# A retention-plus-FFN kernel on one Trainium2 core: a new hand-written order for the first 32 FFN slots, and steps over two PSUM banks merged

## The chip, the cores and the metric

The kernel runs on one core of a Trainium2 chip. The metric is device time in microseconds (us), the median of three runs; lower is better. The engines are named as the profile names them: PE (TensorE matmul) and PEld (its weight loads), DVE (VectorE), ACT (ScalarE), POOL (GpSimd) and SP (SyncE, which issues nearly all DMAs here). Each engine works through its own list of instructions in order; semaphores connect the lists.

## The reference

For 4 batches, 8 heads, 768 tokens and head size 64, a retention layer with a decay per head feeds a feed-forward network whose nonlinearity is a rational function. Everything is float32.

```python
state = gamma * state + k[t] (outer) v[t]          # 64 x 64 per head, token by token
y[t]  = scale * q[t] @ state
x = y of all heads, as [3072 tokens, 512]
h = x @ w_in                                       # 512 -> 2048
P = a[0] + a[1]*h + a[2]*h**2 + a[3]*h**3
Q = 1 + |b[0]|*|h| + |b[1]|*h**2
out = (P / (Q + 1e-6)) @ w_out                     # 2048 -> 512
```

## The kernel before

**Retention.** Tokens are taken in 24 chunks of 128 (six to a batch). For a chunk i the steps are, with the letters that the order below uses: load (four DMAs on SP's queue: v, k, kT, qT), q and v (scale qT and v by decays, one POOL step each), S (scores, k times q, on PE), M (multiply by the causal mask, DVE, out of PSUM), V (mask times v, PE), R and r (recall from the state, PE), O (outer product of k and v for the state, PE), C (add the state, DVE), s (decay it, POOL), X (round the result to the PE's fast float format, ACT: the high part xh) and Y (the remainder xl, DVE). Chunks 0 to 3 work on whole chunks of 128 tokens; from chunk 4 on a chunk is done in two halves of 64, whose scores and results lie in two PSUM banks, the tile `pair`. There is one such tile, so that S of a chunk waits for Y of the chunk before it. M, X and Y are two instructions each, one for each bank.

**FFN.** Four chunks make a block of 512 tokens; there are six blocks and 16 slices of 128 of the hidden dimension, so 96 slots. Each slot has gemm_in (letter I, `gemm_in`, L480) of 12 matmuls of 512 columns: high and low part of x against high and low part of the weight; the rational function; and gemm_out (letter Z, `gemm_out`, L536) of 12 more. For slot 0 gemm_in comes in two cuts, I0 (384 columns) and J0 (128). Between I and Z lie, per slot: a = absolute value (ACT), b = affine (ACT, or POOL where the list says `b...!`), c = linear (ACT), p = product (POOL), f = two DVE steps (L504, L505), e = two ACT steps (reciprocal square root, square), H = three DVE steps (L513, L514, L515), g = high part of the result (ACT), K = low part (POOL). I of a slot k writes one of two banks `ph`, and so it waits until H of slot k-2 has read its bank; Z of a slot waits for its K.

**Weights.** w_in and w_out come as 64-bit floats and are decoded on the chip, a tile of [128, 512] at a time, 32 tiles in all: fetch (DMA on SP), t and u (ACT), d (two DVE steps, L160 and L163), h (high part, ACT) and l (low part, POOL). Scratch for u lies in a PSUM bank that is free at that time; the name after @ says which. Slots 0 to 7 are block 0 against the first half of the hidden dimension, slots 8 to 15 block 1 against the same weights, slots 16 to 31 the same two blocks against the second half. Slots 0 to 7 need tiles 0 to 15, slots 16 to 23 tiles 16 to 31; slots 8 to 15 and 24 to 31 need no new ones. Slot 32 and the later ones belong to blocks 2 to 5.

**Who sets the order.** All instructions stand in an order written out by hand; nothing reorders them. Up to slot 31 it is the text BEGIN, one word to a step (letter and number; `fillN` is N dummy matmuls on zeros; `fetch1` the next weight tile; `loadN` a chunk; w, y and sums store and reload partial sums). An exclamation mark moves the step to its other engine: for q, v, l, p and K from POOL to DVE, for b from ACT to POOL. From slot 32 on the loop `run` gives a regular order. SP's queue is in the order of the text as well; 11 weight tiles and chunks 0 to 5 are issued ahead of BEGIN.

Of the kernel before, what the change touches and what calls it, by code (L numbers as in the profile page):

```python
# [21 lines left out]
def tile_retention_rational_ffn(  # L22
# [111 lines left out]

    def decode_low(i):
        if i >= len(tiles):
            return
# [4 lines left out]
        nc.scalar.activation(ts[i], byte, AF.Identity, bias=lcon[:, 0:1], scale=1.0 / 32)
# [24 lines left out]
    def decode_split(i):  # L167
# [5 lines left out]
        nc.scalar.copy(w[:, 0], ts[i].bitcast(F32))  # L173
# [241 lines left out]
    def mask(i, ordered=False):  # L415
        st = steps[i]
        for r in range(2):
            st["aT", r] = at.tile([P, NP, HP], F32, name="aT")
            x = nc.vector.tensor_mul(
                st["aT", r], st["pa"][r],  # L420
                causal_sb[:, :HP].unsqueeze(1).broadcast_to([P, NP, HP]),
            )
# [25 lines left out]
    def x_parts(i, kh):  # L448
        n, s = divmod(i, SPB)
        t = slice(s * P + kh * HP, s * P + (kh + 1) * HP)  # L450
        xh, xl = (y[:, :, t] for y in x_block(n))
        return pair(i)[kh][:, TB // 2 :].rearrange("p (n t) -> p n t", t=HP), xh, xl

    def x_high(i, r):
        x, xh, _ = x_parts(i, r)
        nc.scalar.copy(xh, x)

    def x_low(i, r):
        x, xh, xl = x_parts(i, r)
        nc.vector.tensor_sub(xl, x, xh.bitcast(F32))  # L460
# [51 lines left out]
    def ratio_vector(ph, p, q, s):  # L512
        nc.vector.scalar_tensor_tensor(q, q, qcon[:, 0:1], ph, ALU.add, ALU.mult)  # L513
        nc.vector.scalar_tensor_tensor(ph, p, par_sb[:, 0:1], ph, ALU.add, ALU.mult)  # L514
        nc.vector.scalar_tensor_tensor(p, q, 2.0, ph, ALU.subtract, ALU.mult, reverse0=True)  # L515
# [298 lines left out]
t0 B0 u0@ph1 d0 h0 q0 l0 fill20 S0 v0 M0 v1 fill2 O0 V0 C0 q1 O1 X0 n0 s1 S1 t1 Y0 u1@po2 C1 R1  # L814
M1 s2 d1 fill1 V1 X1 v2! h1 q2! fill1 O2 l1 Y1 S2 C2 t2 s3 R2 M2 u2@ph1 v3 d2 fill1 V2 q3 O3 X2
h2 C3 S3 Y2 t3 s4 l2 u3@po2 R3 M3 I0 v4 d3 q4 V3 h3 t4 l3 O4 X3 C4 t5 v5 u4@po2 Y3 u5@po0 d4 s5
fill4 J0 S4 a0 q5 d5 h4 I1 c0 l4 t6 f0 h5 fetch1 b0! u6@po1 l5 R4 t7 d6 a1 p0 u7@po2 M4 h6 d7 t8
fill4 V4 b1! c1 r4 l6 O5 load6 u8@po0 C5 f1 X4 p1 t9 h7 Y4 u9@po1 l7 fetch1 d8 fill6 S5 e0 R5 v6
M5 h8 H0 t10 fill2 V5 l8 e1 r5 O6 load7 q6 u10@po2 H1 fill1 I2 t11 X5 g0 fetch1 u11@po0 C6 K0 g1
d9 I3 a2 K1 c2 Y5 b2 v7 d10 h9 p2 S6 a3 fetch1 f2 R6 h10 s7 c3 l10 b3 M6 e2 d11 fill4 V6 q7 r6  # L820
O7 load8 f3 h11 p3 Z0 X6 C7 l9 e3 Y6 fetch1 s8 t12 H2 S7 l11 t13 Z1 v8 t14 H3 g2 q8 R7 K2 fetch1
I4 M7 g3 u12@half0 K3 d12 Z2 a4 u13@half0 b4 d13 fetch1 c4 p4 h12 I5 f4 h13 l12 u14@half0 e4 d14
l13 Z3 t15 H4 fetch1 a5 u15@half0 b5! c5 p5 d15 h14 I6 g4 t16 K4 f5 h15 u16@half0 fetch1 l15
l14! e5 Z4 d16 t17 H5 a6 t18 b6! V7 c6 p6 r7 h16 fetch1 O8 f6 g5 I7 l16 X7 load9 K5! e6 Y7 C8
t19 Z5 a7 H6 s9 fetch1 u17@pair0 b7! c7 v9 u18@pair1 f7 g6 I8 p7 d17 q9 fetch1 e7 K6 d18 h17 Z6
a8 u19@pair0 l17 H7 b8 fetch1 c8 p8 t20 f8 I9 g7 u20@pair1 K7 h18 d19 e8 fetch1 l18 Z7 d20 a9
t21 b9! c9 H8 p9 h20 fetch1 h19 S8 l20 w8 R8 f9 I10 g8 l19 y8 e9 K8 fetch1 M8 t22 Z8 H9 a10 t23
b10! c10 p10 u21@half0 f10 I11 g9 fetch1 K9 d21 e10 Z9 u22@half0 H10 a11 h21 fetch1 b11! c11 l21
d22 g10 I12 p11 t24 f11 u23@half0 K10 h22 fetch1 d23 e11 Z10 l22 a12 H11 u24@half0 b12! c12 p12
fetch1 t25 f12 h23 I13 g11 l23 d24 e12 K11 fetch1 t26 Z11 H12 a13 h24 b13! c13 l24 p13!  # L830
u25@half0 I14 g12 f13 t27 K12 d25 e13 Z12 a14 H13 h25 b14 l25 c14 u26@half0 p14 I15 f14 t28 g13
d26 e14 K13 Z13 a15 H14 h26 b15! c15 l26 u27@half0 f15 g14 I16 p15 t29 d27 e15 K14! Z14
u28@half0 H15 a16 h27 c16 l27 b16 f16 I17 g15 p16 t30 d28 K15 e16 Z15 a17 H16 h28 b17! c17 p17
u29@half0 f17 g16 I18 w16 K16 l28! e17 y16 Z16 t31 H17 a18 b18 c18 p18 d29 I19 g17 f18 u30@half0
h29 l29 sums0 K17! Z17 e18 d30 a19 H18 c19 b19 V8 h30 r8 p19 O9 load10 f19 g18 I20 l30 C9 e19
K18 H19 Z18 a20 v10 c20 s10 b20 f20 g19 p20 I21 q10! K19 e20 H20 Z19 a21 b21 c21 p21 g20 f21 I22
K20 e21 H21 Z20 a22 b22 c22 p22 g21 f22 I23 K21 e22 H22 Z21 X8 a23 b23 Y8 c23 p23 g22 I24 f23
u31@pair0 K22 d31 e23 Z22 a24 H23 h31 c24 l31 b24 f24 g23 p24 S9 I25 K23 e24 H24 R9 a25 Z23 b25
c25 M9 p25 g24 f25 K24 V9 y24 e25 I26 H25 r9 a26 Z24 b26 c26 p26 g25 f26 load11 O10 K25! Z25 e26
C10 X9 H26 s11 v11 I27 Y9 g26 q11 K26 S10 a27 I28 b27 c27 p27 f27 R10 a28 Z26 M10 e27 c28 H27  # L840
b28 V10 p28 r10 O11 f28 load12 g27 I29 X10 K27 Y10 e28 C11 v12 H28 S11 a29 Z27 c29 b29 f29 g28
p29 K28! R11 e29 I30 q12! M11 H29 V11 a30 r11 c30 b30! O12 load13 g29 f30 p30 I31 X11 K29 Y11
# [69 lines left out]
```

## Time and profile before

| | |
|---|---|
| median of 3 runs | 621.27 us (621.22 to 621.86) |
| the profiled execution | 621.15 us, with a span of 619.1 us |
| PE busy | 606.9 us, 98% of the span |
| DVE, ACT, POOL busy | 453.9, 441.8 and 346.5 us (73%, 71%, 56%) |
| granted TensorE clock | 1.0 throughout |
| matmuls of gemm_in and gemm_out | 1164 and 1152 |

The span is the time from the first to the last instruction of the program; the time of a run has some 2 us beside it. The busy share of PE holds the dummy matmuls too, and matmuls whose modelled end is late. The shares are averages: the first sixth of the span, where the weights are decoded and the first chunks are made, and the rest, where PE has a full list, have different limits.

### The profile page before, as it was taken

What the parts mean: (1) busy time and instruction counts of PE and PEld (TensorE: products, weight loads), DVE (VectorE), ACT (ScalarE), POOL (GpSimd) and SP (SyncE); (2) the same over time, 40 slices, a digit from 0 to 9 for tenths busy, and PEclk for the clock granted to TensorE, in tenths of its full rate; (3) what the DMA queues carried; (4) which work ended last, traced back from release to release, by engine and by line L of the source; (5) the groups of instructions that cost most, each with busy time, mean ns of one, the idle gap of its engine ahead of it and who ended that gap; (6) DMA issues with size and microseconds to landing.
All of it is one profiled execution on the core that took longest, in us unless ns stands there. A gap on an engine that the chain in (4) does not pass through costs nothing.

```text
span 619.1 us, 12618 instructions
## 1 busy us (share of the span) xinstructions
PE 606.9 (98%) x5044; PEld 487.6 (79%) x5050; DVE 453.9 (73%) x717; ACT 441.8 (71%) x723; POOL 346.5 (56%) x296
## 2 busy tenths in 40 slices
PE   8979999999999999999999999999999999999997
PEld 5757877887887788888888888888888888888886
DVE  4799899999868686766766766666767666766664
ACT  3598889998675666676666757666766667777773
POOL 4789687865654455464545545554646444444441
PEclk9999999999999999999999999999999999999999
DMA  8977265103203240420120320110301000100001
GB/s 333 387 236 266 110 239 225 48 1 136 69 2 128 70 137 1 137 69 19 53 60 1 137 69 2 69 46 25 137 10 53 1 1 1 68 1 0 2 0 68
DMA packets 24283, 52.87 MB, mean 85 GB/s; under 512 B 2721, under 2 KB 3105, under 8 KB 24225
## 3 DMA queue, kind: packets, MB, share of 16 engines
q1 hardware_dynamic: 24080, 51.94, 23.7%
q8 instruction: 39, 0.64, 0.4%
q14 instruction: 20, 0.16, 0.1%
q10 hardware_dynamic: 144, 0.13, 0.1%
HBM read 43.67 MB, written 8.39 MB: 84 GB/s over the span
## 4 chain that ended last, share of the span: by engine, by line
PE 83%; DVE 3%; issue 1%; ACT 1%; DVEq 0%; ACTq 0%
PE po L536 39%; PE ph L480 39%; PE pair L442 2%; PE pair L394 2%; PE pair L409 1%; PE pair L283 1%; DVE q L513 0%; DVE t L163 0%; DVE pair L160 0%; DVE ph L514 0%; DVE p L515 0%; DVE p L504 0%; DVE w L180 0%; DVE p L505 0%; ACT s L629 0%
## 5 line engine op out<-in xcount | busy, mean ns | idle before, releaser
L480 PE MATMUL ph<-xh,w 128*128 128x512 f32 (+2 forms) x776 | 210.0, 393 | 1.6 <-DVE p L515 1.3
L536 PE MATMUL po<-w,gh 128*128 128x512 f32 x768 | 200.1, 393 | 0.0
L499 POOL TENSOR_TENSOR q<-q,s 128x512 f32<-128x512 f32 x64 | 83.1, 1298 | 183.9 <-ACT s L498 183.9
L480 PEld LDWEIGHTS ph<-xh,w 128*128 128x128 f32 x776 | 142.9, 188 | 33.6 <-DVE p L515 4.1
L536 PEld LDWEIGHTS po<-w,gh 128*128 128x128 f32 x768 | 142.7, 188 | 30.3
L504 DVE TENSOR_TENSOR p<-ph,p 128x512 f32<-128x512 f32 x96 | 66.2, 690 | 85.4 <-ACT p L500 75.5
L536 PE MATMUL po<-w,gl 128*128 128x512 f32 x384 | 110.7, 390 | 0.0
L480 PE MATMUL ph<-xl,w 128*128 128x512 f32 (+2 forms) x388 | 103.7, 389 | 0.1
L513 DVE SCALAR_TENSOR_TENSOR q<-q,qcon,ph 128x512 f32<-128x512 f32 x96 | 71.5, 745 | 40.9 <-ACT ph L510 39.8
L492 ACT ACTIVATE q<-ph 128x512 f32<-128x512 f32 x64 | 38.3, 598 | 87.8 <-PE ph L480 87.8
L480 PEld LDWEIGHTS ph<-xl,w 128*128 128x128 f32 x388 | 72.7, 188 | 15.7 <-DVE xl L382 0.2
L509 ACT ACTIVATE s<-q,qcon 128x512 f32<-128x512 f32 x96 | 69.5, 724 | 21.0 <-POOL q L499 14.0
L536 PEld LDWEIGHTS po<-w,gl 128*128 128x128 f32 x384 | 72.1, 188 | 15.4 <-POOL gl L646 0.5
L521 POOL TENSOR_TENSOR gl<-p,gh 128x512 fp32r<-128x512 f32 x64 | 82.8, 1294 | 0.5 <-POOL q L499 0.5
L505 DVE SCALAR_TENSOR_TENSOR p<-p,con_sb,ph 128x512 f32<-128x512 f32 x96 | 71.8, 748 | 3.4
L514 DVE SCALAR_TENSOR_TENSOR ph<-p,con_sb,ph 128x512 f32<-128x512 f32 x96 | 71.9, 749 | 0.0
L515 DVE SCALAR_TENSOR_TENSOR p<-q,ph 128x512 f32<-128x512 f32 x96 | 65.9, 687 | 3.3
L510 ACT ACTIVATE ph<-s 128x512 f32<-128x512 f32 x96 | 57.8, 602 | 10.8 <-DVE p L505 1.4
L633 POOL TENSOR_TENSOR q<-q,s 128x512 f32<-128x512 f32 x31 | 40.1, 1293 | 31.5 <-ACT s L629 28.2
L498 ACT ACTIVATE s<-q,babs 128x512 f32<-128x512 f32 x64 | 52.3, 817 | 2.1
L500 ACT ACTIVATE p<-ph,con_sb 128x512 f32<-128x512 f32 x64 | 48.8, 763 | 0.0
L180 POOL TENSOR_TENSOR w<-t,w 128x512 fp32r<-128x512 f32 x30 | 39.3, 1313 | 14.5 <-ACT w L173 14.5
(75 smaller groups left out, 615.1 us busy)
## 6 DMA issues: line engine op xcount, KB each, us to landing
raw<-in_w_in SPq DMA_DIRECT2D x16, 512.0 KB, 7.5
raw<-in_w_out SPq DMA_DIRECT2D x16, 512.0 KB, 6.9
kT<-in_kT SPq DMA_DIRECT2D x24, 256.0 KB, 3.9
qT<-in_qT SPq DMA_DIRECT2D x24, 256.0 KB, 4.1
v<-in_v SPq DMA_DIRECT2D x24, 256.0 KB, 3.3
out<-o SPq DMA_DIRECT2D x23, 256.0 KB, 2.2
...
```

The costliest lines, as they stand in the source:

```text
L480: nc.tensor.matmul(ph[:, t0:t1], w1[f][:, part, kt * P : (kt + 1) * P], x[:, kt, t0:t1], start=(i == 0), stop=(i == 3 * NP - 1),)
L498: nc.scalar.activation(s, q, AF.Identity, bias=babs[:, 0:1], scale=babs[:, 1:2])
L499: nc.gpsimd.tensor_mul(q, q, s)
L504: nc.vector.tensor_mul(p, ph, p)
L505: nc.vector.scalar_tensor_tensor(p, p, par_sb[:, 1:2], ph, ALU.add, ALU.mult)
L509: nc.scalar.activation(s, q, AF.Abs_reciprocal_sqrt, bias=qcon[:, 0:1])
L510: nc.scalar.activation(ph, s, AF.Square)
L513: nc.vector.scalar_tensor_tensor(q, q, qcon[:, 0:1], ph, ALU.add, ALU.mult)
L514: nc.vector.scalar_tensor_tensor(ph, p, par_sb[:, 0:1], ph, ALU.add, ALU.mult)
L515: nc.vector.scalar_tensor_tensor(p, q, 2.0, ph, ALU.subtract, ALU.mult, reverse0=True)
L521: engine.tensor_sub(gl, p, gh.bitcast(F32))
L536: nc.tensor.matmul(o_tiles[n][tt], g_[:, tt * P : (tt + 1) * P], w2[f][:, part], start=(first and m == 0), stop=(last and m == 2),)
```

## The change

The change has four parts.

1. **A new text BEGIN.** The same steps stand in a new order on every engine. There are 20 dummy matmuls after the first twenty instead of 26. Tiles 16 to 31 are decoded later. No q, v, l, p or K step is left on DVE (before: v2, q2, q10, q12, l14, l28, p13, K5, K14, K17, K25, K28), b on POOL is down from 13 slots to 7, and three steps go from ACT to POOL: t20, t25 and h10. The two texts are, up to gemm_in of slot 12:

```
before
t0 B0 u0@ph1 d0 h0 q0 l0 fill20 S0 v0 M0 v1 fill2 O0 V0 C0 q1 O1 X0 n0 s1 S1 t1 Y0 u1@po2 C1 R1 M1
s2 d1 fill1 V1 X1 v2! h1 q2! fill1 O2 l1 Y1 S2 C2 t2 s3 R2 M2 u2@ph1 v3 d2 fill1 V2 q3 O3 X2 h2 C3
S3 Y2 t3 s4 l2 u3@po2 R3 M3 I0 v4 d3 q4 V3 h3 t4 l3 O4 X3 C4 t5 v5 u4@po2 Y3 u5@po0 d4 s5 fill4 J0
S4 a0 q5 d5 h4 I1 c0 l4 t6 f0 h5 fetch1 b0! u6@po1 l5 R4 t7 d6 a1 p0 u7@po2 M4 h6 d7 t8 fill4 V4 b1!
c1 r4 l6 O5 load6 u8@po0 C5 f1 X4 p1 t9 h7 Y4 u9@po1 l7 fetch1 d8 fill6 S5 e0 R5 v6 M5 h8 H0 t10
fill2 V5 l8 e1 r5 O6 load7 q6 u10@po2 H1 fill1 I2 t11 X5 g0 fetch1 u11@po0 C6 K0 g1 d9 I3 a2 K1 c2
Y5 b2 v7 d10 h9 p2 S6 a3 fetch1 f2 R6 h10 s7 c3 l10 b3 M6 e2 d11 fill4 V6 q7 r6 O7 load8 f3 h11 p3
Z0 X6 C7 l9 e3 Y6 fetch1 s8 t12 H2 S7 l11 t13 Z1 v8 t14 H3 g2 q8 R7 K2 fetch1 I4 M7 g3 u12@half0 K3
d12 Z2 a4 u13@half0 b4 d13 fetch1 c4 p4 h12 I5 f4 h13 l12 u14@half0 e4 d14 l13 Z3 t15 H4 fetch1 a5
u15@half0 b5! c5 p5 d15 h14 I6 g4 t16 K4 f5 h15 u16@half0 fetch1 l15 l14! e5 Z4 d16 t17 H5 a6 t18
b6! V7 c6 p6 r7 h16 fetch1 O8 f6 g5 I7 l16 X7 load9 K5! e6 Y7 C8 t19 Z5 a7 H6 s9 fetch1 u17@pair0
b7! c7 v9 u18@pair1 f7 g6 I8 p7 d17 q9 fetch1 e7 K6 d18 h17 Z6 a8 u19@pair0 l17 H7 b8 fetch1 c8 p8
t20 f8 I9 g7 u20@pair1 K7 h18 d19 e8 fetch1 l18 Z7 d20 a9 t21 b9! c9 H8 p9 h20 fetch1 h19 S8 l20 w8
R8 f9 I10 g8 l19 y8 e9 K8 fetch1 M8 t22 Z8 H9 a10 t23 b10! c10 p10 u21@half0 f10 I11 g9 fetch1 K9
d21 e10 Z9 u22@half0 H10 a11 h21 fetch1 b11! c11 l21 d22 g10 I12

after
t0 B0 u0@ph1 q0 v0 fill20 S0 v1 O0 M0 C0 fill2 V0 d0 q1 O1 X0 n0 s1 S1 h0 Y0 v2 t1 C1 R1 M1 u1@po2
s2 O2 d1 V1 q2 X1 C2 l0 S2 t2 Y1 u2@ph1 M2 v3 R2 h1 s3 d2 fill1 V2 q3 O3 X2 h2 Y2 S3 t3 v4 u3@po2 R3
M3 l1 C3 fill3 V3 d3 s4 l2 O4 X3 I0 C4 t4 q4 Y3 u4@po2 h3 d4 s5 t5 S4 l3 R4 u5@po0 J0 M4 h4 v5 d5 a0
V4 c0 r4 l4 O5 I1 C5 X4 f0 q5 t6 u6@po1 Y4 b0! h5 d6 t7 p0 S5 load6 a1 R5 u7@po2 M5 l5 e0 d7 fill2
V5 r5 t8 fetch1 H0 c1 v6 b1 load7 fill7 O6 u8@po0 p1 f1 g0 I2 h6 q6 X5 C6 e1 fetch1 Y5 l6 d8 h7 S6
a2 K0 R6 t9 M6 h8 v7 H1 fill3 V6 u9@po1 r6 c2 l7 O7 load8 b2 f2 s7 g1 fill1 I3 p2 t10 X6 d9 fetch1
K1 e2 C7 Z0 l8 a3 Y6 h9 H2 c3 q7 u10@pair0 b3 l9 fetch1 t11 d10 fill1 I4 p3 t12 f3 u11@pair1 h10! g2
u12@pair0 v8 d11 Z1 e3 l10 fetch1 d12 a4 h11 K2 t13 H3 S7 b4 l11 R7 c4 Z2 h12 s8 M7 g3 p4 f4 t14
fetch1 u13@half0 K3 I5 d13 e4 l12 H4 h13 V7 a5 r7 c5 b5! O8 load9 t15 f5 p5 I6 X7 g4 C8 e5 K4 fetch1
Y7 Z3 a6 H5 c6 b6 u14@pair0 p6 f6 I7 u15@pair1 g5 l13 d14 fetch1 e6 K5 H6 Z4 a7 b7 c7 p7 t16 f7 I8
fetch1 g6 h14 K6 d15 e7 s9 H7 l14 Z5 a8 fetch1 c8 b8 f8 h15 p8 u16@pair0 I9 g7 d16 l15 e8 fetch1 K7
t17 H8 Z6 a9 c9 b9! t18 p9 f9 fetch1 u17@pair1 I10 u18@pair0 d17 e9 h16 H9 fetch1 l16 Z7 a10 h17 g8
d18 b10 K8 g9 I11 y8 t19 l17 fetch1 c10 w8 p10 f10 u19@pair1 Z8 K9 e10 d19 fetch1 t20! a11 H10 h18
c11 Z9 l18 u20@pair0 h19 f11 b11! fetch1 t21 p11 u21@pair1 d20 I12
```

The PE steps of slots 22 to 28 show how the small retention matmuls stand among the large ones:

```
before  Z22 S9 I25 R9 Z23 V9 I26 r9 Z24 O10 Z25 I27 S10 I28 R10 Z26 V10 r10 O11 I29 S11 Z27 R11 I30 ...
after   Z22 S9 R9 I25 Z23 I26 V9 r9 O10 Z24 I27 Z25 I28 Z26 S10 R10 I29 V10 r10 O11 Z27 I30 S11 R11 I31 ...
```

2. **Steps over two banks merged.** M (from chunk 4 on), X and Y become one instruction over both banks. This holds in `run` too.

```diff
-        for r in range(2):
-            st["aT", r] = at.tile([P, NP, HP], F32, name="aT")
-            x = nc.vector.tensor_mul(
-                st["aT", r], st["pa"][r],
-                causal_sb[:, :HP].unsqueeze(1).broadcast_to([P, NP, HP]),
-            )
-            if ordered and r == 1:
-                after(x, st["recalled"])
+        aT = at.tile([P, 2, NP, HP], F32, name="aT", bufs=1)
+        for r in range(2):
+            st["aT", r] = aT[:, 1 - r]
+        x = nc.vector.tensor_mul(
+            aT, both_banks(i)[:, :, : TB // 2].rearrange("p b (n t) -> p b n t", t=HP),
+            causal_sb[:, :HP].unsqueeze(1).unsqueeze(1).broadcast_to([P, 2, NP, HP]),
+        )
+        if ordered:
+            after(x, st["recalled"])
...
-    def x_high_both(i):
-        for r in range(2):
-            x_high(i, r)
+    def x_high(i):
+        x, xh, _ = x_parts(i)          # both banks
         nc.scalar.copy(xh, x)
```

3. **An immediate in place of a per-partition constant** in the first step of H, in all 96 slots:

```diff
-        nc.vector.scalar_tensor_tensor(q, q, qcon[:, 0:1], ph, ALU.add, ALU.mult)
+        nc.vector.scalar_tensor_tensor(q, q, 1.0 + 1e-6, ph, ALU.add, ALU.mult)
```

4. **Other engines for t, h, g and the stores**, where the text marks them:

```diff
-    def decode_low(i):
+    def decode_low(i, engine=None):
...
-        nc.scalar.activation(ts[i], byte, AF.Identity, bias=lcon[:, 0:1], scale=1.0 / 32)
+        if engine is None:
+            nc.scalar.activation(ts[i], byte, AF.Identity, bias=lcon[:, 0:1], scale=1.0 / 32)
+        else:
+            engine.tensor_scalar(
+                ts[i], byte, 1.0 / 32, -15.5 / 32, op0=ALU.mult, op1=ALU.add
+            )
...
+                other = {"w": nc.vector.tensor_copy, "y": nc.scalar.copy}
+                other.update({x: nc.gpsimd for x in "bthg"})
+                more.append(other.get(word[0], nc.vector))
```

More of the change, by code (lines that the diff above doesn't have):

```diff
@@ L69, in pair @@
             pairs[i] = [both[:, r] for r in range(2)]
+            boths[i] = both
             if i >= SPB:
@@ L72, in pair, with both_banks @@
         return pairs[i]
+    def both_banks(i):
+        pair(i)
+        return boths[i]
     def u_place(i, place):
@@ L129, in tile_retention_rational_ffn, with round_to @@
     us, ts = {}, {}
+    def round_to(dst, src, engine=None):
+        if engine is None:
+            nc.scalar.copy(dst, src)
+        else:
+            engine.tensor_copy(dst, src)
     def decode_read(i, place=None):
@@ L165, in decode_join, with decode_split @@
         )
-    def decode_split(i):
+    def decode_split(i, engine=None):
         if i >= len(tiles):
@@ L365, in whole_values, with whole_x @@
                     )
-    def whole_x(i, r):
+    def whole_x(i):
         t = slice((i % SPB) * P, (i % SPB + 1) * P)
         xh, xl = (
-            y.rearrange("p (a r) t -> p a r t", r=2)[:, :, r, t] for y in x_block(i // SPB)
+            y.rearrange("p (a r) t -> p r a t", r=2)[:, :, :, t] for y in x_block(i // SPB)
         )
-        return whole_px(i, r), xh, xl
+        x = both_banks(i)[:, :, : TB // 2].rearrange("p r (a t) -> p r a t", t=P)
+        return x, xh, xl
     def whole_x_high(i):
-        for r in range(2):
-            x, xh, _ = whole_x(i, r)
-            nc.scalar.copy(xh, x)
+        x, xh, _ = whole_x(i)
+        nc.scalar.copy(xh, x)
     def whole_x_low(i):
-        for r in range(2):
-            x, xh, xl = whole_x(i, r)
-            nc.vector.tensor_sub(xl, x, xh.bitcast(F32))
+        x, xh, xl = whole_x(i)
+        nc.vector.tensor_sub(xl, x, xh.bitcast(F32))
     def px(i, kh):
@@ L446, in values, with x_parts, x_low @@
                         )
-    def x_parts(i, kh):
+    def x_parts(i):
         n, s = divmod(i, SPB)
[L450 to L455, printed above, removed]
+        xh, xl = (
+            y[:, :, s * P : (s + 1) * P].rearrange("p n (k t) -> p n k t", k=2)
+            for y in x_block(n)
+        )
+        x = both_banks(i)[:, :, TB // 2 :].rearrange("p k (n t) -> p n k t", t=HP)
+        return x, xh, xl
+    def x_high(i):
+        x, xh, _ = x_parts(i)
         nc.scalar.copy(xh, x)
-    def x_low(i, r):
-        x, xh, xl = x_parts(i, r)
+    def x_low(i):
+        x, xh, xl = x_parts(i)
         nc.vector.tensor_sub(xl, x, xh.bitcast(F32))
-    def x_high_both(i):
-        for r in range(2):
-            x_high(i, r)
-    def x_low_both(i):
-        for r in range(2):
-            x_low(i, r)
         del steps[i]
@@ L553, in store_last, with store @@
             queue.dma_start(out=dst[:, cut], in_=o[:, cut])
-    def store(n, half, which=range(SPB)):
+    def store(n, half, which=range(SPB), copy=None):
         for tt in which:
@@ L650, in load_chunk, with store_group @@
             load_by_dim(i)
-        def store_group(k, which):
+        def store_group(k, which, copy=None):
             n, f = order[k - 1]
-            store(n, f // HF, range(*which))
+            store(n, f // HF, range(*which), copy)
         emit = {
@@ L753, in run @@
                 carry(chunk + 1)
-                x_high_both(chunk)
+                x_high(chunk)
                 if not summed:
-                    x_low_both(chunk)
+                    x_low(chunk)
                 load_by_token(chunk + 2)
@@ L770, in run @@
             if part == 1 and summed:
-                x_low_both(chunk)
+                x_low(chunk)
             if plain:
@@ L813 @@
 BEGIN = """
[L814 to L842, printed above, removed]
@@ L843 @@
-e30 C12 v13 Z28 a31 H30 b31 s13 c31 p31 f31 g30 K30 e31 H31
+t0 B0 u0@ph1 q0 v0 fill20 S0 v1 O0 M0 C0 fill2 V0 d0 q1 O1 X0 n0 s1 S1 h0 Y0 v2 t1 C1 R1 M1
+u1@po2 s2 O2 d1 V1 q2 X1 C2 l0 S2 t2 Y1 u2@ph1 M2 v3 R2 h1 s3 d2 fill1 V2 q3 O3 X2 h2 Y2 S3 t3
+v4 u3@po2 R3 M3 l1 C3 fill3 V3 d3 s4 l2 O4 X3 I0 C4 t4 q4 Y3 u4@po2 h3 d4 s5 t5 S4 l3 R4 u5@po0
+J0 M4 h4 v5 d5 a0 V4 c0 r4 l4 O5 I1 C5 X4 f0 q5 t6 u6@po1 Y4 b0! h5 d6 t7 p0 S5 load6 a1 R5
+u7@po2 M5 l5 e0 d7 fill2 V5 r5 t8 fetch1 H0 c1 v6 b1 load7 fill7 O6 u8@po0 p1 f1 g0 I2 h6 q6 X5
@@ new lines @@
+C6 e1 fetch1 Y5 l6 d8 h7 S6 a2 K0 R6 t9 M6 h8 v7 H1 fill3 V6 u9@po1 r6 c2 l7 O7 load8 b2 f2 s7
+g1 fill1 I3 p2 t10 X6 d9 fetch1 K1 e2 C7 Z0 l8 a3 Y6 h9 H2 c3 q7 u10@pair0 b3 l9 fetch1 t11 d10
+fill1 I4 p3 t12 f3 u11@pair1 h10! g2 u12@pair0 v8 d11 Z1 e3 l10 fetch1 d12 a4 h11 K2 t13 H3 S7
+b4 l11 R7 c4 Z2 h12 s8 M7 g3 p4 f4 t14 fetch1 u13@half0 K3 I5 d13 e4 l12 H4 h13 V7 a5 r7 c5 b5!
+O8 load9 t15 f5 p5 I6 X7 g4 C8 e5 K4 fetch1 Y7 Z3 a6 H5 c6 b6 u14@pair0 p6 f6 I7 u15@pair1 g5
+l13 d14 fetch1 e6 K5 H6 Z4 a7 b7 c7 p7 t16 f7 I8 fetch1 g6 h14 K6 d15 e7 s9 H7 l14 Z5 a8 fetch1
@@ new lines @@
+c8 b8 f8 h15 p8 u16@pair0 I9 g7 d16 l15 e8 fetch1 K7 t17 H8 Z6 a9 c9 b9! t18 p9 f9 fetch1
+u17@pair1 I10 u18@pair0 d17 e9 h16 H9 fetch1 l16 Z7 a10 h17 g8 d18 b10 K8 g9 I11 y8 t19 l17
+fetch1 c10 w8 p10 f10 u19@pair1 Z8 K9 e10 d19 fetch1 t20! a11 H10 h18 c11 Z9 l18 u20@pair0 h19
+f11 b11! fetch1 t21 p11 u21@pair1 d20 I12 g10 e11 K10 d21 fetch1 l19 H11 Z10 a12 h20 b12! c12
+p12 t22 f12 g11 I13 fetch1 u22@pair0 K11 h21 d22 e12 l20 Z11 H12 a13 h22 b13! c13 fetch1 p13 t23
+f13 u23@pair1 I14 l22 g12 d23 e13 K12 fetch1 H13 l21 Z12 a14 h23 c14 b14! t24 p14 f14 g13 fetch1
@@ new lines @@
+I15 u24@pair0 t25! e14 d24 l23 u25@pair1 H14 K13 Z13 a15 b15 c15 p15 t26 f15 I16 h24 g14 d25 e15
+K14 l24 H15 Z14 a16 c16 b16 f16 u26@pair0 p16 g15 I17 t27 d26 K15 u27@pair1 h25 d27 q8 e16 Z15
+a17 H16 c17 b17 S8 w16 p17 f17 R8 I18 g16 l25 h27 M8 e17 y16 K16 H17 Z16 a18 v9 b18 c18 p18 t28
+f18 I19 g17 u28@half0 K17 e18 l27 H18 Z17 a19 h26 c19 l26 b19 f19 g18 p19 I20 t29 d28 K18 e19
+u29@half0 Z18 H19 a20 c20 b20 f20 t30 p20 I21 g19 d29 K19 e20 q9 H20 Z19 a21 h28 c21 l28 b21 f21
+t31 p21 I22 g20 K20 e21 Z20 H21 a22 u30@half0 c22 h29 d30 b22 I23 p22 f22 h30 g21 l29 e22 V8 l30
@@ new lines @@
+r8 a23 H22 O9 load10 K21 Z21 X8 c23 C9 b23 Y8 s10 g22 I24 f23 p23 u31@pair0 K22 d31 e23 Z22 a24
+H23 h31 b24 l31 sums0 c24 g23 p24 S9 f24 R9 I25 q10 M9 e24 K23 H24 Z23 a25 c25 g24 f25 b25 I26
+p25 y24 v10 e25 K24 V9 a26 H25 r9 O10 load11 c26 Z24 b26 f26 p26 g25 K25 C10 e26 I27 s11 H26 Z25
+a27 c27 b27 f27 X9 p27 g26 I28 Y9 v11 e27 K26 H27 Z26 a28 b28 p28 g27 c28 S10 q11 f28 R10 I29
+K27 M10 e28 H28 V10 a29 r10 b29 O11 load12 Z27 c29 p29 g28 f29 X10 K28 C11 e29 Y10 I30 v12 H29
+S11 a30 R11 c30 I31 M11 g29 f30 b30 p30 V11 K29 e30 r11 O12 load13 q12 Z28 X11 H30 a31 c31 b31
@@ L844 @@
+f31 g30 p31 Y11 K30 e31 C12 s13 H31 v13
 """
```

21 lines of the change are left out of this document (11 added, 10 removed).

## The prediction

> **What bounds the kernel now.** I took the time by stages first. The columns are the busy time of PE, PEld, DVE, ACT and POOL (with instructions), the granted clock, the DMA share and GB/s.
>
> ```profile
> 8.10:30.00 21.90, 20.03 (x303) 16.07 (x305) 16.00 (x32) 10.40 (x22) 17.07 (x18) 1.00 1.04 391
> 30.00:98.00 68.00, 62.71 (x749) 48.50 (x753) 62.94 (x104) 61.65 (x108) 55.76 (x50) 1.00 0.55 199
> 98.00:228.00 130.00, 129.87 (x966) 103.61 (x967) 111.06 (x172) 101.86 (x169) 77.79 (x66) 1.00 0.27 94
> 228.00:604.50 376.50, 376.50 (x2965) 308.26 (x2964) 255.07 (x396) 258.45 (x411) 191.57 (x158) 1.00 0.12 41
> ```
>
> From 98 us on PE has no idle time to win: 0.13 us up to slot 31, none in the loop. A new order can gain there only by making PE's own list cheaper. PE's idle time lies ahead: 1.9 us between 8 and 30 us, where the DMA engines are full (1.04), and 5.3 us between 30 and 98 us. In that stretch DVE is busy 93% of the time and ACT 91%, while PE's busy time holds dummies too. So it is DVE and ACT work with PE waiting. The chain of waits names which of the two:
>
> ```profile
> PE pair L409 <- DVE xl L460: 1.4, 1, 1.4
> PE ph L480 <- DVE p L515: 1.3, 3, 0.6
> ```
>
> The columns are total, times and longest, in us. Both releasers are DVE. What counts is when the three steps of H are through, since they open the bank for gemm_in two slots later.
>
> **Start and data.** S0 follows the same 20 dummies; the first 11 weight tiles and six chunks are queued ahead of BEGIN as before. Then load6, load7 and load8 each move on SP ahead of a fetch that they stood behind, and tiles 13 and 14 now wait behind load8, that is, until chunk 6 is done (V6, r6, O7). I cost this at nothing: t13 stands on ACT behind a4, which waits for gemm_in of slot 4, while V6 precedes I3. More than a slot covers it, with the DMA engines 55% busy. If V6 came later than that, tile 13 would be late next.
>
> **DVE, step by step.** A stretch of DVE's timeline without a gap (start, duration) gives prices from start to start:
>
> ```profile
> 75.85 0.69 DVE L160 SCALAR_TENSOR_TENSOR pair<-pair,t 128x512 uint32<-128x512 uint32 x1
> 76.63 0.69 DVE L163 SCALAR_TENSOR_TENSOR t<-raw,pair 128x512 uint32<-128x512 uint32 x1
> 77.23 0.74 DVE L513 SCALAR_TENSOR_TENSOR q<-q,qcon,ph 128x512 f32<-128x512 f32 x1
> 77.89 0.75 DVE L514 SCALAR_TENSOR_TENSOR ph<-p,con_sb,ph 128x512 f32<-128x512 f32 x1
> 78.68 0.69 DVE L515 SCALAR_TENSOR_TENSOR p<-q,ph 128x512 f32<-128x512 f32 x1
> 79.28 0.68 DVE L504 TENSOR_TENSOR p<-ph,p 128x512 f32<-128x512 f32 x1
> 80.00 0.75 DVE L505 SCALAR_TENSOR_TENSOR p<-p,con_sb,ph 128x512 f32<-128x512 f32 x1
> 80.66 0.69 DVE L646 TENSOR_TENSOR gl<-p,gh 128x512 fp32r<-128x512 f32 x1
> 81.27 0.75 DVE L460 TENSOR_TENSOR xl<-pair,xh 128x256 fp32r<-128x256 f32 x2
> ```
>
> d costs 1.38 (77.23 - 75.85), H 2.05, f 1.38, and one 512-column step such as K on DVE 0.61; I take that for q2 and v2 too. The pair of Y (x2) takes 0.75 for two; one step of 512 columns should take the 0.69 of its neighbours. So merging saves 0.06, no more, since the pair overlapped already, and a mask, a pair of the same form, likewise. One read over two banks has no row: between a gain of 0.06 and a loss of as much a step, the eleven that matter make plus or minus 0.7; I take the gain, as the 512-column rows are the nearest. X merged counts as nothing. The immediate makes L513 like L515, which has one: 0.74 to 0.69, so 0.05 per H.
>
> Two ends of H in the old order:
>
> ```profile
> 58.01 0.69 DVE L515 SCALAR_TENSOR_TENSOR p<-q,ph 128x512 f32<-128x512 f32 x1
> ...
> 70.89 0.69 DVE L515 SCALAR_TENSOR_TENSOR p<-q,ph 128x512 f32<-128x512 f32 x1
> ```
>
> H2 ended at 58.7. Counted in the two texts, DVE now has ahead of it d for 10 tiles in place of 12 (2.76), f for 3 slots in place of 4 (1.38), no q2 and v2 (1.22), 10 merged M and Y (0.6) and three immediates (0.15): 6.1 less. With DVE's other gaps as they were, H2 ends at 52.6.
>
> H4 ended at 71.6. One d less (1.38), q2 and v2 (1.22), 11 merges (0.66), five immediates (0.25): 3.5 less, 68.1. But between H3 and H4 DVE idled for these:
>
> ```profile
> DVE pair L160 <- ACT pair L150: 1.9, 2, 1.1
> DVE aT L419 <- PE pair L394: 0.3, 1, 0.3
> ```
>
> The 0.3 is M7 waiting for R7; 0.8 of the 1.9 is d12, whose u12 waits for the half bank that M7 frees. The new order decodes u11 and u12 in `pair` ahead of S7, so this 1.1 goes. The other 1.1, u13, still follows M7 and stays. H4 ends at 67.0; 68.1 if nothing goes, 65.9 if all goes.
>
> **PE from there.** The price of a gemm (chain, start and length) and places in PE's timeline:
>
> ```profile
> 106.50 2.72 PE po L536 x12
> ```
> ```profile
> 94.01 0.62 PE L536 MATMUL po<-w,gh 128*128 128x512 f32 x2
> ...
> 97.88 1.20 PE L480 MATMUL ph<-xh,w 128*128 128x512 f32 x4
> ...
> 109.06 1.07 PE L480 MATMUL ph<-xh,w 128*128 128x512 f32 x4
> ...
> 150.99 1.98 PE L536 MATMUL po<-w,gh 128*128 128x512 f32 x8
> ...
> 155.13 1.20 PE L480 MATMUL ph<-xh,w 128*128 128x512 f32 x4
> ...
> 179.74 1.98 PE L536 MATMUL po<-w,gh 128*128 128x512 f32 x8
> ...
> 197.01 1.20 PE L536 MATMUL po<-w,gh 128*128 128x512 f32 x4
> ```
>
> A gemm takes 2.72. Z7, S8 and R8 take 97.88 - 94.01 = 3.87, so S and R in a row cost 1.15, of which 0.13 is PE's only idle time here: 1.02. Z17, V8, r8 and O9 take 4.14: V, r, O cost 1.42.
>
> In the new order I4 starts with H2's end, 52.6; Z1 at 55.3; after S7 R7, Z2 at 59.0; I5 at 61.8. V7 r7 O8 end at 65.9, and I6 waits for H4 until 67.0. From I6 to I12 lie 13 gemms, 35.4 us, and no small work: I12 at 102.4. Later H stay ahead by the same count (before H7 DVE has three d, l14, K5, q2 and v2 less). The old I12 starts at 109.06 with S8 and R8 done, which the new list does after Z15; the place to compare is 107.9. **First term: 5.5 us gained** (4.4 and 6.6 at the two ends for H4). K and l back on POOL delay Z by up to one POOL step, covered by the gemm_in that stands between H and Z.
>
> **Second term, the small matmuls.** From Z22 to Z25 the old order has five gemms with S9, R9, V9, r9 and O10 one by one between them: 197.01 - 179.74 = 17.27, less 13.60, is 3.67. As S R and V r O they cost 1.02 + 1.42 = 2.44; 1.23 gained for three breaks, 0.41 a break. Chunks 10 and 11 lose one break each, R behind S. **2.0 us in all,** and on the path, since PE is full there. What could take it back is the set of sums: loaded after Z22 and not slot 19, added by y24 on DVE (four steps) ahead of Z24. Two gemms and V9 r9 O10 lie between Z23's start and Z24, 6.9 us; that covers them.
>
> The rest is nothing: the merged steps and immediates of the loop lie under a PE busy 376.50 of 376.50 us. The sum is 7.5. The profiled execution took 621.15, 0.12 below the median of the runs; 621.15 - 7.5 = 613.7 (rounded up), its own range 612.5 to 615.
>
> **Rivals.**
>
> *ACT takes DVE's place.* By line, in the stretch from 30 to 140 us (count, busy, mean ns):
>
> ```profile
> L142 ACT ACTIVATE t<-raw,lcon 128x512 uint32<-128x512 uint8 x25 | 19.0, 763 | 1.1 <-POOL w L180 0.8 <-DVE w L180 0.2
> L173 ACT CAST w<-t 128x512 fp32r<-128x512 f32 x24 | 14.6, 615 | 0.1
> ```
>
> Ahead of e15 ACT has five t, two u and three h less, but four b more, back from POOL: six steps net, at 0.62 to 0.76 some 3.7 to 4.6 us, where DVE sheds nearly 9 by H7 already. If ACT keeps all its idle gaps, e15, and with it H15 and I17, come 3.7 earlier, of which S8 R8, still to do, take 1.15: 2.5 gained, with the second term 4.5, so 616.6. For it: ACT's 91%. Against: part of its gaps are waits for PE and shrink with them. 0.20.
>
> *The waits vanish.* If DVE and ACT keep up, PE's 7.3 us of idle time go, and six dummies:
>
> ```profile
> 37.36 1.47 PE L602 MATMUL fill<-zeros 128*128 128x512 bf16 x5
> ```
>
> At 0.29 each these are 1.8; with the second term 11.1, so 610.0. For it: the new text puts dummies at V5, O6 and V6, where small matmuls follow each other's mask. Against: DVE's list still holds 90% of the stretch. 0.16.
>
> *Slower, by POOL.* No row shows POOL reading bytes, as t20 and t25 now do. The nearest are one input and two inputs of 512 columns:
>
> ```profile
> 31.52 1.30 POOL L180 TENSOR_TENSOR w<-t,w 128x512 fp32r<-128x512 f32 x1 [0.94 <-ACT w L173]
> 32.80 0.77 POOL L626 TENSOR_SCALAR s<-q,babs 128x512 f32<-128x512 f32 x1
> ```
>
> I take 0.77, the row of the same operation. t20 stands ahead of b11 and p11, and so of e11, H11 and I13; t25 likewise of slot 15. POOL is 60% busy from 98 us on, so 2.2 of a slot's 5.4 us cover a slow step. At 7 us each the loss, 2 x (7 - 0.8 - 2.2) = 8.0, passes the gain; at 8 us the time is 613.7 + 10 = 623.7. Nothing in the profile speaks for steps so long; 1.30 would cost nothing. 0.06.
>
> *A hole slows PE.* The first dummies, after an idle PE:
>
> ```profile
> 1.19 6.99 PE L602 MATMUL fill<-zeros 128*128 128x512 bf16 x20 [1.19 <-DVE lcon L784]
> ```
>
> They take 0.35 each, against 0.29 later, so an idle PE restarts slowly, 1.2 us over twenty. With six dummies fewer, a hole of 3 us and a restart would cost some 4 of the 7.5: 617.9. My largest hole is the 1.1 at I6, and after the 1.4 of the waits above the clock stayed 1.00. 0.03. The Trainium skill (TensorE: Matmul & The Clock Gate, Why this matters for your kernels) sets the limit at PE-idle gaps of about 3 us, after which the clock falls to half; the trace agrees in that 1.4 us did no harm, and no run here shows 3. By that rule alone nothing changes below such a hole.
>
> **How the numbers follow.** My forecast has 0.50; 0.05 is left for an early lead that both full lists lose again before slot 16, which ends within 0.2% (1.2 us, about what a measurement of this kernel can tell from no change). Faster: 0.50 + 0.20 + 0.16 + 0.03 = 0.89; same 0.05; slower 0.06. The range goes from the case without waits, 610.0 less half a microsecond, to the slow-PE case, 618.
>
> **What would show it.** DVE without any l, q, v, p or K step; the first step of H at 0.69; masks of 512 columns at 0.69. H2 ending near 52.6, I6 starting near 67 behind the last step of H4, I12 near 102.4, PE without idle time after that; R9 right behind S9; POOL's t near 0.77. I am wrong if ACT's steps, not DVE's, precede the gaps of PE between 50 and 100 us, if I12 comes after 106, or if PE waits again after 110.

## The result, and the profile after

| | before | after |
|---|---|---|
| median | 621.4 us (621.22 to 621.86) | 614.14 us (613.99 to 615.09) |
| ratio | | 0.9885, 95% interval 0.9868 to 0.9902 |
| the profiled execution | 621.15 us, span 619.1 | 613.99 us, span 612.2 |

The change saves 7.3 us. I had forecast 613.7 (own range 612.5 to 615), 0.4 us under the measured time. In the experiments below four executions fell into a slower state (one of a0_after, 1381.72 us, and three of the kernel before, 752.40 to 1213.79 us); they are left out of all ratios and intervals and move no median by more than 0.04 us. The same stages as before, in the changed kernel (busy time of PE, PEld, DVE, ACT and POOL, granted clock, DMA share, GB/s):

```profile
8.10:30.00 21.90, 20.69 (x382) 16.77 (x382) 18.31 (x31) 11.81 (x21) 18.87 (x20) 1.00 1.04 387
30.00:98.00 68.00, 65.96 (x662) 51.87 (x653) 61.53 (x97) 64.09 (x108) 55.09 (x48) 1.00 0.54 194
98.00:228.00 130.00, 129.03 (x1053) 104.70 (x1052) 103.75 (x158) 104.87 (x171) 91.84 (x78) 1.00 0.28 100
228.00:604.50 376.50, 376.50 (x2930) 308.38 (x2929) 249.34 (x371) 257.12 (x397) 190.25 (x156) 1.00 0.12 40
```

PE's idle time from 30 to 98 us fell from 5.3 to 2.0 us. ACT's busy time there rose from 61.65 to 64.09, 94% of the stretch, and is now above DVE's. From 98 to 228 us PE idles 0.97 us, where before it idled 0.13. The waits of PE name where (total, times, longest, in us; the wait ahead of the first dummies, 1.2 us in both kernels, is left out):

```profile
PE pa L344 <- POOL qT L258: 1.2, 2, 1.0
PE ph L491 <- DVE p L526: 1.1, 3, 0.4
PE pair L424 <- DVE xl L479: 0.6, 1, 0.6
PE ph L491 <- DVE xl L479: 0.5, 1, 0.5
PE pair L424 <- DVE t L179: 0.4, 1, 0.4
PE pair L458 <- DVE aT L435: 0.3, 1, 0.3
```

The places that the forecast named, from the timelines of DVE, PE and POOL (start, duration): the last step of H2 and of H4, gemm_in of slots 4, 6 and 12, and t20.

```profile
51.99 0.69 DVE L526 SCALAR_TENSOR_TENSOR p<-q,ph 128x512 f32<-128x512 f32 x1
65.41 0.69 DVE L526 SCALAR_TENSOR_TENSOR p<-q,ph 128x512 f32<-128x512 f32 x1
```
```profile
52.73 0.97 PE L491 MATMUL ph<-xh,w 128*128 128x512 f32 x3
...
66.69 1.19 PE L491 MATMUL ph<-xh,w 128*128 128x512 f32 x4
...
102.19 1.07 PE L491 MATMUL ph<-xh,w 128*128 128x512 f32 x4
```
```profile
98.37 0.66 POOL L156 TENSOR_SCALAR t<-raw 128x512 uint32<-128x512 uint8 x1
```

H2 ends at 52.68 (forecast 52.6), H4 at 66.10 (67.0), gemm_in of slot 12 starts at 102.19 (102.4). Two waits stand behind 110 us that I had not forecast: one ahead of gemm_in of slot 18, one in the middle of gemm_in of slot 32, whose xl matmuls wait for Y11:

```profile
136.18 1.20 PE L491 MATMUL ph<-xh,w 128*128 128x512 f32 x4 [0.34 <-DVE p L526]
```
```profile
221.23 1.21 PE L491 MATMUL ph<-xl,w 128*128 128x512 f32 x4 [0.53 <-DVE xl L479]
```

The lead over the kernel before, read off the starts of gemm_in, is 5.7 us at slot 12 (102.19 against the comparable 107.9) and 7.21 at slot 33, where the loop has begun. From there it stays to the last matmul; 0.3 of it is lost in the last stores, so that the span is 6.9 shorter.

### The profile page after: what moved, and what is told of

It reads as the page before. It is cut to its first block, busy times and chain, and to the rows that moved or that the text cites. A ratio compares the mean times of both kernels' runs of the same rounds, so it can differ in the third digit from the quotient of the medians.

```text
span 612.2 us, 12520 instructions
## 1 busy us (share of the span) xinstructions
PE 602.7 (98%) x5044; PEld 487.2 (80%) x5044; DVE 435.7 (71%) x661; ACT 442.2 (72%) x702; POOL 358.2 (59%) x305
## 4 chain that ended last, share of the span: by engine, by line
PE 84%; ACT 4%; DVE 2%; issue 1%; POOL 1%; DVEq 0%; POOLq 0%; ACTq 0%
PE po L547 40%; PE ph L491 39%; PE pair L458 2%; PE pair L409 1%; PE pair L424 1%; PE pair L299 1%; ACT pair L166 1%; POOL gl L657 1%; ACT s L640 1%; ACT q L632 0%; DVE pair L176 0%; DVE t L179 0%; ACT t L154 0%; ACT gh L138 0%; ACT p L648 0%
## 5 line engine op out<-in xcount | busy, mean ns | idle before, releaser
L510 POOL TENSOR_TENSOR q<-q,s 128x512 f32<-128x512 f32 x64 | 83.5, 1304 | 182.8 <-ACT s L509 182.8
L524 DVE SCALAR_TENSOR_TENSOR q<-q,ph 128x512 f32<-128x512 f32 x96 | 65.8, 685 | 47.6 <-ACT ph L521 45.4
L644 POOL TENSOR_TENSOR q<-q,s 128x512 f32<-128x512 f32 x32 | 41.6, 1299 | 34.8 <-ACT s L640 30.8
L196 POOL TENSOR_TENSOR w<-t,w 128x512 fp32r<-128x512 f32 x32 | 41.3, 1293 | 5.6 <-ACT w L138 5.5
```

Of the source, the lines that this page charges most:

```text
L510: nc.gpsimd.tensor_mul(q, q, s)
L524: nc.vector.scalar_tensor_tensor(q, q, 1.0 + 1e-6, ph, ALU.add, ALU.mult)
```

## The experiments

All times are medians; "before" is the kernel before, run beside them on the same chip. The first four kernels, then the next four, then the last four were run together.

| kernel | us | before | ratio, 95% interval |
|---|---|---|---|
| a0_after: the change again | 614.34 | 621.48 | 0.9884 (0.9869 to 0.9900) |
| e1_old_steps: new order alone | 615.16 | 621.48 | 0.9901 (0.9888 to 0.9915) |
| e2_old_order: the rest alone | 620.70 | 621.48 | 0.9988 (0.9979 to 0.9997) |
| e3_split: four breaks put back | 615.89 | 621.48 | 0.9910 (0.9895 to 0.9925) |
| e10_dve_back: twelve steps on DVE | 614.69 | 621.41 | 0.9888 (0.9874 to 0.9903) |
| e6_act_more: 2.3 us more on ACT, late | 616.54 | 621.41 | 0.9920 (0.9905 to 0.9935) |
| e7_no_fill: no dummies | 614.95 | 621.41 | 0.9890 (0.9873 to 0.9906) |
| e8_act_back: t20, t25, h10 on ACT | 616.16 | 621.41 | 0.9913 (0.9898 to 0.9928) |
| e9_best: two waits taken out | 613.99 | 621.61 | 0.9878 (0.9864 to 0.9892) |
| e11_dve_extra: probe on DVE, early | 620.88 | 621.61 | 0.9989 (0.9979 to 0.9998) |
| e12_act_extra: probe on ACT, early | 615.08 | 621.61 | 0.9896 (0.9882 to 0.9910) |
| e13_pool_extra: probe on POOL, early | 615.43 | 621.61 | 0.9903 (0.9887 to 0.9919) |

An interval is some 1.8 us wide, so differences of less than a microsecond between two rows are read from the profiles: the start of a gemm_in in one against the same gemm_in in a0_after. One thing has to be taken off first. PE's wait for chunk 3's scores (its qT) was 0.1 to 1.4 us from run to run, and shifts all behind it; I therefore take the lag at slot 3 (47 us) off.

**Order or steps.**

> The changed kernel once more, beside the experiments of this group: 614.0 to 614.4 us, span near 612.2. The others are compared with it by the times at which gemm_in of each slot starts.

For e1 the functions of M, X and Y and the first line of H are those of before (first edit); for e2 only the text BEGIN is (second edit; the table of other engines is the old one too, but the old text uses none of its new entries):

```diff
-        nc.vector.scalar_tensor_tensor(q, q, 1.0 + 1e-6, ph, ALU.add, ALU.mult)
+        nc.vector.scalar_tensor_tensor(q, q, qcon[:, 0:1], ph, ALU.add, ALU.mult)
...
-BEGIN = """ (new order)
+BEGIN = """ (old order)
```

> The new order, but mask, X and Y in two instructions and the first step of H with the per-partition constant again. Theory (the order carries the gain, through the DVE work ahead of H): H2 ends 0.75 us later (10 pairs at 0.06, 3 constants at 0.05), I4 with it, and the end 0.5 to 1.2 us later than the changed kernel, so 614.6 to 615.4. Rival (the merged steps carry it): at least 3 us later, 617 or more. Second rival (PE alone, nothing of DVE matters): no difference.

> The old order with the merged steps and the immediate. Theory: 1.1 us of DVE work less ahead of H7 (12 pairs, 8 constants), of which PE's waits at I7 and I9 (0.56 and 0.42) and a little before give back 0.5 to 1.3 us: 620.0 to 620.8, all of it before slot 10. Rival (the merged steps carry the gain): 617 or less.

The order alone saves 6.3 us, the merged steps and the immediate alone 0.8; together 7.1. Within the noise they add up, and the order carries the gain.

**The small matmuls.**

```diff
-S9 f24 R9 I25 q10 M9 e24 K23 H24 Z23
+S9 f24 I25 R9 q10 e24 K23 H24 M9 Z23
-a26 H25 r9 O10 load11 c26 Z24 b26 f26 p26 g25 K25 C10 e26 I27 s11 H26 Z25
+a26 H25 c26 Z24 r9 b26 f26 p26 g25 K25 e26 I27 O10 load11 H26 C10 s11 Z25
-K26 H27 Z26 a28 b28 p28 g27 c28 S10 q11 f28 R10 I29
+K26 H27 S10 Z26 a28 b28 p28 g27 c28 q11 f28 R10 I29
```

> The new order, but four of the five breaks between small and large matmuls put back: R9 behind I25 and not behind S9, r9 behind Z24 and O10 behind I27 and not behind V9, S10 ahead of Z26 and not in front of R10. Theory: 0.41 us a break, so 1.3 to 1.9 us later than the changed kernel, all between slots 24 and 30: 615.4 to 616.2. Rival (small matmuls hide beside the large ones either way): within 0.3 us of the changed kernel.

Four breaks cost 1.55 us, 0.39 each; I had taken 0.41.

**DVE's list.** Here my theory was that DVE's list ahead of H2 sets gemm_in of slot 4, with all of q2, v2, d and f in it.

```diff
-v2 ... q2 ... K5 ... l14 ... p13 ... q10
+v2! ... q2! ... K5! ... l14! ... p13! ... q10!
```

> The new order, with the twelve steps q2, v2, q10, q12, l14, l28, p13, K5, K14, K17, K25 and K28 on DVE again. Theory (DVE's list ahead of H2 sets gemm_in of slot 4 and everything behind it): v2 and q2 add 2 x 0.61 = 1.2 us ahead of H2, so H2 ends near 53.9 and not 52.7, and the time rises by 0.6 to 1.4 us above 614.34, to 614.9 to 615.7; the other ten steps lie where H is ahead of PE and add nothing. Rival (ACT or PE's own list sets this stretch): within 0.3 us of 614.34.

By the medians e10 came 0.35 us above, between theory and rival, and at the place that it was made for the theory missed. In the DVE timeline of e10 the two steps (L264, L258) and the last step of H2:

```profile
12.52 0.68 DVE L264 TENSOR_TENSOR v<-v,con_sb 128x512 f32<-128x512 f32 x1
...
15.97 0.69 DVE L258 TENSOR_TENSOR qT<-qT,qdec_sb 128x512 f32<-128x512 f32 x1
...
22.15 1.29 DVE L353 TENSOR_TENSOR aT<-pa,con_sb 128x512 f32<-128x512 f32 x2 [0.44 <-PE pa L344]
...
52.27 0.69 DVE L526 SCALAR_TENSOR_TENSOR p<-q,ph 128x512 f32<-128x512 f32 x1
```

Gemm_in of slot 4 starts at 53.02, in a0_after at 53.00. The mask of chunk 3 (22.15 us) waits for its scores in both, 0.44 us here and 0.92 in a0_after; what DVE does ahead of it is free as long as some of that wait is left. So in the new order the list that counts begins at chunk 3's mask, not at the start. The 0.6 us that the gemms of e10 do lose come between slots 14 and 18; half of that does not show in the time, as the last stores took 0.3 us less in that execution.

Three probes at one place, ahead of slot 2's steps, then asked each engine for its spare time:

```diff
-O7 load8 b2 f2 s7 g1 fill1 I3 p2
+O7 load8 b2 D6 f2 s7 g1 fill1 I3 p2     (e11: six products on DVE)
+O7 load8 A4 b2 f2 s7 g1 fill1 I3 p2     (e12: four absolute values on ACT)
+O7 load8 b2 f2 s7 g1 fill1 I3 P4 p2     (e13: four products on POOL)
```

> The new order, with six needless products of 128 columns on DVE (some 1.2 us) ahead of f2, two steps ahead of H2. First of three probes of one size at one place, one to an engine. Theory (DVE's list sets gemm_in of slot 4): 0.8 to 1.2 us above 614.34, and gemm_in of slot 4 as much later. Rival (another engine sets it): 0 to 0.3.

> The new order, with four needless absolute values of 128 columns on ACT (4 x 0.325 = 1.3 us) ahead of b2, at the place of the DVE probe. DVE alone: within 0.3 us of 614.34. DVE first and ACT just behind it (ACT idles under 0.3 us from 40 to 52.7): 0.3 to 0.9 us above, by u10 and u12, which DVE waits for. Both lists equally full: 1.0 to 1.3 above.

> The new order, with four needless products of 128 columns on POOL (some 1.3 us) ahead of p2, at the place of the other two probes. POOL has no gap from 39.3 to 64.4 us, but its results there are needed 1.4 us or more after they are made. Theory: within 0.2 us of 614.34. Rival (a list without gaps is a bound): 1.0 us or more above.

The probes and what they did, from the timelines of each kernel: DVE and PE of e11, then DVE of e12, then POOL and DVE of e13.

```profile
47.24 6.02 DVE L707 TENSOR_TENSOR extra<-qdec_sb 128x128 f32<-128x128 f32 x6
...
58.66 0.69 DVE L528 SCALAR_TENSOR_TENSOR p<-q,ph 128x512 f32<-128x512 f32 x1
```
```profile
56.03 1.22 PE L549 MATMUL po<-w,gh 128*128 128x512 f32 x2 [4.88 <-DVE t L181]
...
60.13 2.08 PE L493 MATMUL ph<-xh,w 128*128 128x512 f32 x4
```
```profile
56.86 0.70 DVE L178 SCALAR_TENSOR_TENSOR pair<-pair,t 128x512 uint32<-128x512 uint32 x1 [0.86 <-ACT pair L168]
```
```profile
46.83 1.83 POOL L707 TENSOR_TENSOR extra<-qdec_sb 128x128 f32<-128x128 f32 x4
```
```profile
51.42 0.69 DVE L526 SCALAR_TENSOR_TENSOR q<-q,ph 128x512 f32<-128x512 f32 x1 [0.71 <-ACT ph L523]
```

- **DVE:** the probe came out at 5.94 us (47.24 to 53.18) and not 1.2; why is told below. H2 ended at 59.35 against 52.95, 6.4 later, of which 0.47 were there at slot 3: 5.93. Each microsecond on DVE reaches H2. The gemms behind lag 7.1 us (7.57 less 0.47), 1.2 more than the probe.
- **ACT:** 1.22 us of probe, 0.3 of lag at slot 4 and 0.8 from slot 5 on; the middle case. The second part goes by u11: DVE's d11 waits 0.86 us for it where it waited 0.40 in a0_after, d12 follows d11, and S7 waits for d12.
- **POOL:** 1.79 us of probe, 0.8 of lag at slot 4 and 1.5 from slot 5 on. My expectation failed. POOL's p2 feeds ACT's e2, which had started 0.12 us after p2's end in a0_after (48.44, 48.56), and the first step of H2 now waits 0.71 us for e2.

So the theory "DVE alone" falls: seen from slot 5, at this place DVE has no spare time, POOL 0.3 us and ACT 0.4.

**ACT from slot 10 on.**

```diff
-K9 e10 d19
+K9 A7 e10 d19
```

> The new order, with seven needless absolute values of 128 columns on ACT ahead of e10, some 1.5 to 2 us of ACT work where PE is about to have a full list (90 to 96 us). Theory (DVE set the start, and ACT has gaps behind it): ACT catches up in its own gaps; 0 to 0.7 us above 614.34. Rival (ACT's list takes DVE's place from there): all of it reaches H10 and gemm_in of slot 12, 1.5 us or more above 614.34.

```diff
-h10! ... t20! ... t25!
+h10 ... t20 ... t25
```

> The new order, with t20, t25 and h10 on ACT again and not on POOL. Theory: h10 on ACT delays u12, which S7 waits for through d12, by some 0.5 us, and t20 and t25 fall into gaps of ACT: +0.3 to +0.7 us against 614.34. Rival (ACT is the bound from slot 4 on): all three steps, 0.62 + 2 x 0.76 = 2.1 us, less what ACT's small gaps take: +1.5 us or more.

Both went the rival's way. The seven steps of e6 took 2.28 us (98.04 to 100.32), and the lag grew by 2.2: 0.76 at slot 12, the rest at slots 13 and 14, with PE waiting for H behind ACT's e10 and e11. ACT's and PE's timelines of e6:

```profile
98.04 2.37 ACT L707 ACTIVATE extra<-qdec_sb 128x128 f32<-128x128 f32 x7
100.32 0.71 ACT L522 ACTIVATE s<-q,qcon 128x512 f32<-128x512 f32 x1
```
```profile
103.90 1.19 PE L493 MATMUL ph<-xh,w 128*128 128x512 f32 x4 [0.60 <-DVE p L528]
...
110.69 0.50 PE L493 MATMUL ph<-xh,w 128*128 128x512 f32 x1 [1.05 <-DVE p L528]
```

In e8 the lag grows by 0.5 at slot 5 (h10, by u12 and S7, as expected), 0.7 at slots 13 to 15 (t20) and 0.3 at slot 18 (t25): 1.5 of 2.1 us of moved work in the profile, 1.8 by the medians.

**Dummies.**

> The new order, without any dummy matmul after the first twenty. Theory: the dummies only fill PE's waits, whose ends other engines set, and the holes that open (1 to 2 us) are too short to slow PE: -0.3 to +0.2 us against 614.34. Rival (a hole slows PE, as its restart after the start of the program does): +1 us or more, with a granted clock under 1.00 or gemms above 2.72 us behind the holes.

The edit drops every `fillN` behind the first. PE's timeline of e7, and two stretches of it (columns as above; the clock is third from the end):

```profile
36.45 0.69 PE L458 MATMUL pair<-aT,v 64*64 64x64 f32 x32 [0.81 <-DVE aT L435]
...
38.33 0.69 PE L299 MATMUL pair<-v,k 64*64 64x64 f32 x32 [0.95 <-POOL v L264]
39.95 1.30 PE L491 MATMUL ph<-xh,w 128*128 128x512 f32 x4 [0.93 <-DVE p L526]
41.05 1.91 PE L491 MATMUL ph<-xl,w 128*128 128x512 f32 x4
```
```profile
35.60:40.00 4.40, 1.70 (x85) 1.40 (x81) 4.23 (x8) 4.37 (x8) 1.98 (x3) 1.00 0.97 356
41.00:44.00 3.00, 3.00 (x8) 2.30 (x7) 2.33 (x5) 2.56 (x5) 3.00 (x4) 0.50 0.88 296
```

Three holes, none of them a full microsecond, halved the clock from about 41 to 44 us, and gemm_in took 1.91 us for four matmuls where it takes 1.08. That cost 0.8 us at slot 3, and 0.6 by the medians. The rival was right in kind, if not in size. It did not happen in every execution: three of the four took 614.87 to 615.50 us with a mean clock of 0.997, the fourth 614.37 with 0.999, as fast as a0_after.

**A better version.**

```diff
-H30 a31 c31 b31 f31 g30 p31 Y11 K30
+H30 Y11 a31 c31 b31 f31 g30 p31 K30
-K15 u27@pair1 h25 d27 q8 ... R8 I18 g16 l25 h27 M8 e17 y16 K16 H17 Z16 a18 v9 b18 c18 p18
+K15 h25 q8 ... R8 I18 g16 l25 M8 u27@half0 e17 y16 K16 H17 d27 Z16 a18 v9 b18 c18 h27 p18
```

> The new order with two of its own waits taken out: the remainder of chunk 11 (Y11) goes right behind H30, and u27, d27 and h27 go behind M8. Theory: the 0.5 us wait inside gemm_in of slot 32 goes, and the 0.35 us one ahead of gemm_in of slot 18; 613.4 to 613.7 us against 614.34. Rival (u27 behind M8 makes another wait, or slot 32 waits for something else): 614.0 to 614.4.

The forecast missed, at the edge of the rival. Both waits went, and one came in their place, ahead of gemm_in of slot 20: h27 on ACT waits 1.16 us for d27, and e18 and H18 come later.

```profile
148.38 1.19 PE L491 MATMUL ph<-xh,w 128*128 128x512 f32 x4 [0.96 <-DVE p L526]
```

The last matmul ends 0.26 us before that of a0_after. The lowest median of all, 613.99 us, is ahead of both kernels, but its interval overlaps that of the change. Moving Y11 alone was not run; by the lags it is worth 0.8, since from gemm_in of slot 32 to that of slot 33 a0_after takes 7.20 us and e9 6.37.

## Why the forecast was right, and where its steps were not

**DVE's list, 5.5 us: the sum held, its account did not.** Up to H2's end DVE was busy 45.62 us before and 39.85 after: 5.8 less, of 6.1 counted, and its idle time in all hardly moved (13.1 and 12.8). But e10 shows that in the new order the 1.2 us of q2 and v2 are worth nothing. From the start of chunk 3's mask to H2's end (the third figure of these rows is DVE's busy time) it looks otherwise:

```profile
22.64:58.70 36.06, 31.43 (x541) 23.84 (x547) 32.07 (x60) 31.63 (x58) 32.57 (x31) 1.00 0.78 270
```
```profile
21.87:52.68 30.81, 29.16 (x505) 21.82 (x505) 28.05 (x47) 26.32 (x45) 28.31 (x26) 1.00 0.88 311
```

The first row is the kernel before, the second the changed one. DVE's busy time fell by 4.0 us (two d and one f less, the merged steps and immediates, but one C more), its idle time by 1.2 (4.0 to 2.8), and the mask itself starts 0.8 earlier. I had credited q2 and v2 with 1.2 us and taken the gaps as fixed. Both were wrong, and it is luck that they cancel. That DVE is the bound to H2 stands: e11 gave 5.93 of 5.94. That it was the two d and the f which moved H2 is argued from these sums; no run put them back. Nor was H2 the bound in the kernel before: there gemm_in of slot 4 starts 2.21 us behind it (60.91), after Z0, Z1 and R7, and in the changed kernel 0.05 behind it.

**H4, 67.0: 0.9 early.** I let u13's 1.1 us stand. In the new list d13 follows f4, which covers u13: DVE does not wait between H3 and H4, and what is left, 0.41 us for u11, lies ahead of H3. H4 at 66.10 is no longer what opens gemm_in of slot 6: PE comes there from V7, r7 and O8.

**PE has nothing to win from 98 us on: 0.6 wrong.** In the kernel before, the first four matmuls of gemm_in of slots 13 and 15 took 1.20 us and not 1.07, with no idle time recorded, though they start only 0.05 us behind the end of H11 and of H13. Slot 13's:

```profile
114.69 1.20 PE L480 MATMUL ph<-xh,w 128*128 128x512 f32 x4
115.73 1.08 PE L480 MATMUL ph<-xl,w 128*128 128x512 f32 x4
```

That is a wait for H shorter than the modelled end of the last matmul; each of the two costs 0.3 us with its first group. From slot 12 to slot 17 a slot took up to 5.63 us, after the change 5.44; the lead grows by 0.6.

**The grouped matmuls, 2.0 us: about 1.9.** The direct figure is e3's, 0.39 each, so 1.9 for five breaks. What is left of the lead fits it roughly: 7.21 at slot 33, with the recorded waits for Y11 (0.53) and H16 (0.34) added back, less 5.7 and 0.6, leaves 1.8; with the 0.8 that Y11's wait was worth in e9, 2.1.

**After 110 us: wrong.** I said that a wait there would refute me. It did not touch the mechanism, but it took at least 0.9 us, the recorded idle time, so that a lead of 7.2 and not 8.1 us or more came. That 7.2 lies so near the 7.5 counted is luck in part: this loss and the unforeseen 0.6 above nearly cancel. I had followed y24 ahead of Z24 and not Y11, the last step on which block 2 hangs: X11 stands behind e30, Y11 behind f31, and slot 32 is the first to read them.

**Merged steps, immediate: right in sum.** I counted 0.75 ahead of H2; the medians give 0.78 in e2 and 0.82 in e1 for the whole kernel. That the gain lies ahead of H2 is not shown: in e2 H2 ends at 58.69, in the kernel before at 58.70, with gemm_in of slot 3 0.19 later in e2. **t on POOL: right,** 0.66 us, below the 0.77 taken; the slow POOL rival is dead.

**ACT takes DVE's place, given 0.20: nearer than that.** I credited the gain to DVE and left ACT's six steps to the rival. By e8, three of them are worth 1.5 to 1.8 of the 7.1 us; without them the change ends at 616.16 (e8), not far from the rival's 616.6. By e6 ACT has no spare time at slots 11 to 13.

**A hole slows PE, given 0.03: right for this kernel,** as its clock stayed at 1.00; but by the reason that I gave, the longest single hole, e7 would have been safe as well, and was not.
